# One set of strip buffers for a whole three-stage kernel, and conversions and products bound to new places

## The chip, the cores and the metric

The kernel runs on one core of one Trainium2 chip. The metric is device time in microseconds for one execution; the time before is the median of three runs.

## What is computed

Banded attention with four sink columns, then a layer that mixes over tokens and over channels, then the real part of a 2-D Fourier transform, a layer norm and a two-layer MLP. The weights come to the chip as pairs of 32-bit words.

```python
def _attn_ref(q, k, v, n_sink, window):
    scores = scale * np.matmul(q, k.transpose(0, 1, 3, 2))
    keep = is_sink | in_window
    scores = np.where(keep, scores, -1000000000.0)
...
    return np.matmul(a, v).astype(np.float32)

def _moe_ref(x, w_theta, w_tok_r, w_tok_i, w_ch):
    theta = x @ w_theta
    cos_t, sin_t = (np.cos(theta), np.sin(theta))
    zr = x * cos_t
    zi = x * sin_t
    yr = np.einsum('ts,bsd->btd', w_tok_r, zr)
    yi = np.einsum('ts,bsd->btd', w_tok_i, zi)
    u = x + yr + yi
    return u + np.maximum(u @ w_ch, 0.0)

def _moe2_ref(x, w_ch1, w_ch2):
    u = x + np.real(np.fft.fft(np.fft.fft(x, axis=1), axis=2))
...
    ch = np.maximum(un @ w_ch1, 0.0) @ w_ch2
    return (u + ch).astype(np.float32)
```

Two batches, 8 heads of 64, 768 rows, a window of 128; the model width is 512 and the MLP's hidden width 2048.

## The kernel before, in words

**Attention** goes through 12 tiles of 128 rows (2 batches of 6), each in four steps of two heads. A step makes scores on PE, masks them and takes the maximum on DVE (L518), the exponential on ACT (L522), transposes the probabilities on PE into `tp` (L229), evicts them with `rnd` (DVE L210 or ACT L208) and multiplies with v into `oa`; L597 to L599 normalise. In between, `theta_gen` (L765 to L794) makes theta of a finished tile in `th`; its phase is reduced on ACT (L788), DVE (L789, L790) and POOL (L791).

**Sine and cosine** of a tile (b, i) are three ACT instructions in `trig_act` (L800 sine, L801 absolute value, L802 cosine) and two products with x in `trig_mul` (L809), on DVE or POOL.

**Token mixing** (`y_gen`, once for each batch) goes through six tiles j, with a half step for the cosine product and one for the sine product of each. A product is split into a high part (ACT L208) and a low part (L214; DVE for batch 0, POOL for batch 1), and a half step is 24 matmuls into `bank` and three `acc` (512 columns) and two `pc` (256 columns). The generator pauses twice in each half step, so `rest` counts four pauses n for each tile. After this, `chain` runs channel mixing and the Fourier transform (`dft_gen`) of batch 0 between the half steps of batch 1; then comes the MLP.

**Weights** arrive in strips: one DMA, or two, on SP's queue fill a raw buffer of 128x1024 words. `conv` (L270) turns one strip into 128x512 float32: ACT rescales the high words in place (L282), DVE puts the bits together in three steps (L290, L291, L294). Where `self.room` is set, the scratch of the middle steps is a PSUM tile `s`; otherwise it is the target itself, `t`, in SBUF. `split` and `weight_split` make a high and a low part (ACT L208, POOL L214). Token weights have three strips for each tile j, issued in the order 0, 2, 1.

**What sets the order.** Tile's scheduler lays the instructions out on each engine by a model of times and by dependences that only set order. `paced(lag, ref)` gives what is issued inside it such a dependence on a given instruction, or on the matmul `lag` back; `issue_after` does the same for the trigonometry. `pump` (L324) converts the next strip that has been fetched, and then `ahead` (L319) issues further ones as raw buffers are free.

**Raw buffers before.** Attention has three (`raw0` to `raw2`, in its own pool, L397), and stage two opens three others (`rawb0` to `rawb2`, L1176). By 113.11 us the DMAs of all strips of token weights 0 to 3 have been issued, and the strips of weights 0 to 2 are converted within attention. The three strips of weight 3 lie in `raw` until stage two opens; it converts them at once, with PSUM scratch (the loop at L1178), and only then fetches weights 4 and 5 and the channel strips through `rawb`. In `rest`, the pauses n below 2, and those with n mod 4 in `P3S = (1, 3)`, convert one strip each, paced 24 matmuls back.

Of the kernel before, what the change touches and what calls it, by code (L numbers as in the profile page):

```python
# [11 lines left out]
F32 = mybir.dt.float32  # L12
# [23 lines left out]
NRAW1 = 3  # L36
# [13 lines left out]
P3S = (1, 3)  # L50
# [142 lines left out]
class _Body:  # L193
# [11 lines left out]
    def rnd(self, eng, o, i):  # L205
        nc = self.nc
        if eng == "a":
            nc.scalar.activation(o, i, AF.Copy)  # L208
        else:
            nc.vector.tensor_copy(o, i)  # L210
# [137 lines left out]
    def start(self):  # L348
# [17 lines left out]
        self.q, self.v, self.vs, self.ks, self.raw = {}, {}, {}, {}, deque()  # L366
# [28 lines left out]
    def open_attention(self, e, banded):  # L395
        nc = self.nc
        self.raw = deque(e.tile([128, 1024], F32, name=f"raw{k}") for k in range(NRAW1))  # L397
# [136 lines left out]
    def turn(self, n, hp):  # L534
# [20 lines left out]
        self.rnd("v" if tail else EPT[hp], pt[:, 0:k], tp[:, 0:k])  # L555
        self.pt[n, hp] = pt, [(u, m) for u, _, m in parts]
        if hp == 3 and i >= 2:
            tp = self.ps_tp.next()
            self.tr(tp[:, 0:128], self.pt.pop((n, 5)).rearrange("p h c -> p (h c)"), self.ident)
            pst = self.pst.next()  # L560
            self.rnd("v" if tail else "a", pst, tp[:, 0:128])
            self.pt[n, 4] = pst
# [44 lines left out]
    def attn_banded(self):  # L607
        last = len(self.seq) - 1
        nc = self.nc
        self.tn, self.pt, self.scs = {}, {}, {}  # L610
# [4 lines left out]
        for s in range(nstep + T0 + AL + 4):  # L615
# [33 lines left out]
            if s in (nstep + 1, nstep + 3):  # L649
                u = (s - nstep) // 2  # L650
                with self.tc.issue_after(self.last_exp):
                    self.trig_act(0, u)
                self.trig_mul(0, u, "v")
# [27 lines left out]
            elif P0B <= s < P0E and s % P0N == 0:  # L681
                self.pump(12, lag=0, ref=self.last_exp)
            if LA:
                self.mark(LA)
# [120 lines left out]
    def trig_mul(self, b, i, eng="p"):  # L805
        x = self.x.pop((b, i))
        e = self.nc.vector if eng == "v" else self.nc.gpsimd
        for t in self.z[b, i]:
            e.tensor_tensor(t, x, t, op=ALU.mult)  # L809
# [338 lines left out]
    def all(self, banded):  # L1148
# [17 lines left out]
        with ExitStack() as ctx:  # L1166
# [9 lines left out]
            self.raw = deque(e.tile([128, 1024], F32, name=f"rawb{k}") for k in range(NRAW))  # L1176
            self.room = self.ps_s
            for _ in range(len(self.fetched)):  # L1178
                key, raw = self.fetched.popleft()
                self.w[key] = self.conv(raw)  # L1180
            self.raw = deque(list(self.raw)[0:NRAW])
            self.ahead(DEPTH)
            self.room = None
# [7 lines left out]
    def rest(self):  # L1191
        self.sz = self.s.carve(6)
        yg = self.y_gen(0)
        for n, _ in enumerate(yg):
# [8 lines left out]
            if u == 0 and j + 2 < NS:  # L1203
                self.trig_tile(0, j + 2, "v")
            if u == 2 and j < 2:
# [3 lines left out]
            if n < 2 or u in P3S and n < 22:  # L1209
                self.pump(14, lag=24)  # L1210
# [151 lines left out]
```

## Time and profile before

| what | value |
|---|---|
| median of three runs | 619.36 us (617.69 to 619.75) |
| the profiled execution | 619.76 us |
| its span | 617.6 us |
| PE, PE's weight loads | 96%, 84% of the span |
| DVE, ACT, POOL | 57%, 56%, 48% |
| DMA moved | 46.61 MB, mean 75 GB/s |

The profiled execution's own time is 2.2 us above its span and 0.4 us above the median. Busy shares are averages over three stages with different limits. A row of a timeline gives start, busy time, engine, line of the kernel, operation and tile, and in brackets how long the engine was idle before and what released it. The granted clock is a share of PE's full speed. A wait counts where PE, the busiest engine, is the one that waits.

### The profile page before, as it was taken

How to read it: one execution, taken by the hardware profiler on the slowest of the kernel's cores; microseconds unless marked ns; L12 is line 12 of the kernel's file. 1: busy time of each engine (PE TensorE's matmuls, PEld its weight loads, DVE VectorE, ACT ScalarE, POOL GpSimd, SP SyncE). 2: the span in 40 equal slices, each digit the busy share in tenths (PEclk: the TensorE clock that was granted, in tenths of full speed). 3: DMA queues.
4: the chain of work that ended last, by engine and by line, in shares of the span. 5: the costliest groups of instructions: out<-in, count | busy, mean ns of one | idle time of the engine just before them, and what ended most of it. 6: DMA issues, size and time to landing. Idle time of an engine off the chain costs nothing.

```text
span 617.6 us, 9541 instructions
## 1 busy us (share of the span) xinstructions
PE 594.4 (96%) x3490; PEld 521.8 (84%) x3490; DVE 351.4 (57%) x734; ACT 343.2 (56%) x790; POOL 296.4 (48%) x252
## 2 busy tenths in 40 slices
PE   8989999989959999998999999999999999999996
PEld 6868878778848899987899999898899889989985
DVE  5777777754999786585886646746334211121112
ACT  4576766792856443556788854337457433343340
POOL 1122231232845443514565666548758456556551
PEclk9999999999969999998999999999999999999999
DMA  7843351200235612412256710100000000010001
GB/s 245 310 137 120 91 167 54 85 2 1 102 103 162 188 35 70 136 34 70 69 175 195 206 38 2 53 0 1 1 0 27 28 1 1 1 51 1 1 1 57
DMA packets 23337, 46.61 MB, mean 75 GB/s; under 512 B 2512, under 2 KB 9552, under 8 KB 23280
## 3 DMA queue, kind: packets, MB, share of 16 engines
q1 hardware_dynamic: 22032, 43.74, 22.3%
q0 software_dynamic: 1248, 2.17, 1.3%
q8 instruction: 29, 0.48, 0.3%
q14 instruction: 28, 0.23, 0.1%
HBM read 42.75 MB, written 3.15 MB: 74 GB/s over the span
## 4 chain that ended last, share of the span: by engine, by line
PE 81%; DVE 8%; ACT 5%; DMA 2%; issue 1%; SPq 0%; ACTq 0%; DVEq 0%
PE pc L224 26%; PE acc L224 23%; PE s L224 9%; PE bank L224 8%; PE th L224 4%; PE oa L224 4%; PE tp L229 3%; ACT p L522 2%; PE s L229 2%; PE sc L224 2%; DMA raw<-in_w_theta_dram 1%; DVE t L809 1%; ACT t L208 1%; DVE t L290 1%; DVE sc L518 1%
## 5 line engine op out<-in xcount | busy, mean ns | idle before, releaser
L214 POOL TENSOR_TENSOR t<-t 128x512 fp32r<-128x512 f32 x151 | 200.6, 1345 | 185.3 <-ACT t L208 164.3
L224 PE MATMUL pc<-t 128*128 128x384 f32 (+1 forms) x1056 | 199.6, 324 | 0.4 <-ACT t L208 0.4
L224 PEld LDWEIGHTS pc<-t 128*128 128x128 f32 x1056 | 181.6, 189 | 12.1 <-ACT t L208 0.6
L224 PE MATMUL acc<-t 128*128 128x512 f32 x648 | 181.4, 399 | 0.5 <-ACT t L1119 0.5
L208 ACT ACTIVATE t<-t 128x512 fp32r<-128x512 f32 x172 | 102.5, 626 | 98.2 <-PE acc L224 30.2
L224 PEld LDWEIGHTS acc<-t 128*128 128x128 f32 x648 | 117.5, 190 | 19.3 <-ACT t L1119 0.9
L1120 DVE SCALAR_TENSOR_TENSOR t<-pc,t 128x384 fp32r<-128x384 f32 x64 | 35.5, 555 | 130.3 <-ACT t L1119 130.2
L214 POOL TENSOR_TENSOR t<-xT,t 128x512 fp32r<-128x512 f32 x39 | 50.9, 1313 | 53.2 <-ACT xT L775 29.4
L224 PE MATMUL bank<-t 128*128 128x512 f32 x216 | 67.6, 409 | 7.9 <-ACT t L208 6.9
L224 PE MATMUL s<-t 128*128 128x256 f32 (+3 forms) x492 | 69.2, 285 | 0.9 <-DVE st L1040 0.9
L224 PEld LDWEIGHTS s<-t 128*128 128x128 f32 x492 | 65.2, 190 | 3.5 <-DVE st L1040 1.1
L1119 ACT ACTIVATE t<-pc 128x384 fp32r<-128x384 f32 x64 | 31.1, 488 | 57.7 <-PE pc L224 53.3
L224 PEld LDWEIGHTS bank<-t 128*128 128x128 f32 x216 | 39.8, 193 | 16.5 <-ACT t L208 7.9
L224 PEld LDWEIGHTS oa<-t 128*128 128x128 f32 x352 | 45.7, 193 | 2.1 <-ACT p L522 0.8
L224 PE MATMUL oa<-t 128*128 128x64 f32 x352 | 46.8, 264 | 0.4 <-DMA t<-in_v_dram 0.4
L522 ACT ACTIVATE p<-sc,nb 128x272 f32<-128x272 f32 (+1 forms) x72 | 33.1, 468 | 12.8 <-DVE nb L518 12.5
L791 POOL TENSOR_TENSOR t<-t 128x512 f32<-128x512 f32 x12 | 15.6, 1302 | 48.9 <-DVE t L790 41.6
L224 PE MATMUL th<-t 128*128 128x512 f32 x132 | 37.2, 414 | 0.0
L282 ACT ACTIVATE rawb<-rawb 128x512 f32<-128x512 f32 x42 | 28.3, 674 | 12.4 <-DMA rawb<-in_w_ch_dram 7.8
L229 PE MATMUL tp<-ident,p 128*128 128x128 f32 x176 | 33.6, 280 | 0.4 <-DVE t L210 0.4
L518 DVE CUSTOM_DVE_ANT_0 sc<-sc,m 128x272 f32<-128x272 f32 (+1 forms) x72 | 28.6, 443 | 2.7 <-PE sc L224 2.7
L224 PEld LDWEIGHTS th<-t 128*128 128x128 f32 x132 | 23.5, 188 | 7.8 <-issue 2.6
(144 smaller groups left out, 728.2 us busy)
## 6 DMA issues: line engine op xcount, KB each, us to landing
rawb<-in_w_ch_dram SPq DMA_DIRECT2D x36, 512.0 KB, 4.0
kst<-in_k_dram SPq DMA_DIRECT2D x12, 256.0 KB, 3.5
t<-in_v_dram SPq DMA_DIRECT2D x12, 256.0 KB, 4.6
out_dram<-t SPq DMA_DIRECT2D x12, 256.0 KB, 2.5
t<-in_q_dram SPq DMA_DIRECT2D x11, 256.0 KB, 4.7
raw<-in_w_theta_dram SPq DMA_DIRECT2D x4, 512.0 KB, 6.8
raw<-in_w_tok_rT_dram SPq DMA_DIRECT2D x4, 512.0 KB, 3.6
raw<-in_w_tok_iT_dram SPq DMA_DIRECT2D x4, 512.0 KB, 3.9
```

The source lines that it names most:

```text
L208: nc.scalar.activation(o, i, AF.Copy)
L214: e.tensor_tensor(o, x, hi.bitcast(F32), op=ALU.subtract)
L224: i = self.nc.tensor.matmul(o, lhsT=lhsT, rhs=rhs, start=start, stop=stop, skip_group_check=True).ins
L229: self.chained(self.nc.tensor.transpose(o, x, ident).ins)
L282: nc.scalar.activation(hf, hf, AF.Copy, scale=2.0 ** -112)
L290: nc.vector.tensor_scalar(t, hi, 3, None, op0=ALU.logical_shift_left)
L518: nc.vector.tensor_tensor_reduce(out=sc[:, 0:wd], in0=sc[:, 0:wd], in1=mask, op0=ALU.add, op1=ALU.min, scale=-0.125, scalar=3.0e38, accum_ ...
L522: self.last_exp = nc.scalar.activation(p[:, h, 0:wd], sc[:, 0:wd], AF.Exp, bias=nb[:, h:h + 1], scale=-1.0, accum_out=sm[:, h:h + 1]).ins
L791: nc.gpsimd.tensor_tensor(ph, km, ph, op=ALU.subtract)
L809: e.tensor_tensor(t, x, t, op=ALU.mult)
L1119: nc.scalar.activation(hh, hp, AF.Relu)
L1120: self.hl = nc.vector.scalar_tensor_tensor(hl, in0=hp, scalar=0.0, in1=hh.bitcast(F32), op0=ALU.max, op1=ALU.subtract).ins
```

## The change

There is one set of raw buffers for the whole program; `rawb` and the loop that converted the lying strips at stage two's opening are gone. `rnd` returns its instruction, and attention records its evictions in `ev`. In attention's last steps (`TAIL`, counted from the end of the scores) one strip is converted behind each of three evictions, and a split of token weight 1 is issued one step later. The products of tiles (0,0) and (0,1) are bound behind evictions of the last tile. In `rest`, nine pauses (`YC`) convert one strip each, bound behind the last product issued (`tm`), and the splits of the next tile's token weight are issued there too. Lines of the changed kernel are 1 lower up to about L360 and about 5 higher from `theta_gen` on.

```diff
     def rnd(self, eng, o, i):
         nc = self.nc
         if eng == "a":
-            nc.scalar.activation(o, i, AF.Copy)
-        else:
-            nc.vector.tensor_copy(o, i)
+            return nc.scalar.activation(o, i, AF.Copy).ins
+        return nc.vector.tensor_copy(o, i).ins
...
-NRAW1 = 3
-P3S = (1, 3)
+TAIL = (2, 4, 6)
+YC = (1, 3, 5, 9, 11, 13, 17, 19, 21)
...
+        self.raw = deque(cst.tile([128, 1024], F32, name=f"raw{k}") for k in range(NRAW))
...
-        self.raw = deque(e.tile([128, 1024], F32, name=f"raw{k}") for k in range(NRAW1))
...
-        self.rnd("v" if tail else EPT[hp], pt[:, 0:k], tp[:, 0:k])
+        self.ev[n, hp] = self.rnd("v" if tail else EPT[hp], pt[:, 0:k], tp[:, 0:k])
...
                 with self.tc.issue_after(self.last_exp):
                     self.trig_act(0, u)
-                self.trig_mul(0, u, "v")
+                with self.paced(ref=self.ev[last, 1 + u]):
+                    self.trig_mul(0, u, "v")
...
+            if s - nstep in TAIL:
+                self.pump(12, ref=self.ev[last, 1 + (s - nstep) // 2])
+            elif s - nstep - 1 in TAIL:
+                with self.paced():
+                    self.weight_split("tok", 1, TAIL.index(s - nstep - 1))
...
         for t in self.z[b, i]:
-            e.tensor_tensor(t, x, t, op=ALU.mult)
+            self.tm = e.tensor_tensor(t, x, t, op=ALU.mult).ins
...
-            self.raw = deque(e.tile([128, 1024], F32, name=f"rawb{k}") for k in range(NRAW))
-            self.room = self.ps_s
-            for _ in range(len(self.fetched)):
-                key, raw = self.fetched.popleft()
-                self.w[key] = self.conv(raw)
-            self.raw = deque(list(self.raw)[0:NRAW])
             self.ahead(DEPTH)
-            self.room = None
...
             if u == 0 and j + 2 < NS:
                 self.trig_tile(0, j + 2, "v")
+                tm = self.tm
...
-            if n < 2 or u in P3S and n < 22:
-                self.pump(14, lag=24)
+            if n in YC:
+                self.pump(14, ref=tm)
+            if u < 3 and j + 1 < NS:
+                with self.paced(lag=24):
+                    self.weight_split("tok", j + 1, (0, 2, 1)[u])
```

**First place: DVE at the end of attention.** `tp` holds transposed probabilities; t_1499 and t_563 are the two products of tile (0,0), t_1520 and t_665 those of tile (0,1). Before:

```order
L598 RECIPROCAL rs1_180<-rs1_180 128x8
L809 TENSOR_TENSOR t_1499<-t_322,t_1499 128x512
L809 TENSOR_TENSOR t_1520<-t_426,t_1520 128x512
L809 TENSOR_TENSOR t_563<-t_322,t_563 128x512
L210 COPY t_1358<-tp0_206 128x512
L210 COPY pst0_171<-tp1_207 128x128
L789 TENSOR_SCALAR t_1382<-t_1381 128x512
L809 TENSOR_TENSOR t_665<-t_426,t_665 128x512
```

With the change:

```order
L597 RECIPROCAL rs1_180<-rs1_180 128x8
L209 COPY t_1358<-tp0_206 128x512
L209 COPY pst0_171<-tp1_207 128x128
L794 TENSOR_SCALAR t_1382<-t_1381 128x512
L795 TENSOR_SCALAR t_1382<-t_1382 128x512
L209 COPY t_1400<-tp1_207 128x512
L213 TENSOR_TENSOR t_1392<-xT1_71,t_1391 128x512
L598 TENSOR_TENSOR t_1432<-oa0_208,rs0_179 128x512
L209 COPY t_1421<-tp0_206 128x512
L814 TENSOR_TENSOR t_563<-t_322,t_563 128x512
L814 TENSOR_TENSOR t_1499<-t_322,t_1499 128x512
```

The two copies stand directly behind the reciprocal, and the products of tile (0,0) come behind two further copies and a normalisation.

**Second place: DVE in the first token mixing.** t_748 is the cosine product of tile (0,2), t_848 that of (0,3) and t_1282 that of tile (1,1); t_1624, in the changed kernel t_1633, is the sine product of (0,2). Before:

```order
L809 TENSOR_TENSOR t_848<-t_646,t_848 128x512
L291 SCALAR_TENSOR_TENSOR t_1630<-rawb0_1559,t_1630 128x512
L290 TENSOR_SCALAR t_1648<-rawb1_1560 128x512
L294 SCALAR_TENSOR_TENSOR t_1630<-rawb0_1559,t_1630 128x512
L290 TENSOR_SCALAR s1_1552<-rawb2_1561 128x512
L291 SCALAR_TENSOR_TENSOR t_1648<-rawb1_1560,t_1648 128x512
L809 TENSOR_TENSOR t_1624<-t_531,t_1624 128x512
L809 TENSOR_TENSOR t_1282<-t_1104,t_1282 128x512
L291 SCALAR_TENSOR_TENSOR s1_1552<-rawb2_1561,s1_1552 128x512
L214 TENSOR_TENSOR t_1886<-t_848,t_1885 128x512
L294 SCALAR_TENSOR_TENSOR t_1648<-rawb1_1560,t_1648 128x512
L809 TENSOR_TENSOR t_748<-t_531,t_748 128x512
```

With the change:

```order
L814 TENSOR_TENSOR t_1633<-t_531,t_1633 128x512
L289 TENSOR_SCALAR t_1651<-raw1_109 128x512
L290 SCALAR_TENSOR_TENSOR t_1651<-raw1_109,t_1651 128x512
L289 TENSOR_SCALAR s0_1582<-raw2_110 128x512
L814 TENSOR_TENSOR t_748<-t_531,t_748 128x512
L293 SCALAR_TENSOR_TENSOR t_1651<-raw1_109,t_1651 128x512
L814 TENSOR_TENSOR t_1714<-t_646,t_1714 128x512
L290 SCALAR_TENSOR_TENSOR s0_1582<-raw2_110,s0_1582 128x512
L794 TENSOR_SCALAR t_1628<-t_1627 128x512
L289 TENSOR_SCALAR s1_1583<-raw0_108 128x512
L213 TENSOR_TENSOR t_1785<-t_748,t_1784 128x512
```

The products of tiles (0,3) and (1,1) now follow those of (0,2), and three conversion steps stand between the two products of (0,2); before, seven conversion steps and two products of other tiles stand ahead of its cosine product in this piece. The steps that write to t have their scratch in SBUF, those that write to s in PSUM.

**Third place: ACT in the same stretch.** t_1282, t_848 and t_748 are first the phases and then the cosines of the same three tiles. Before:

```order
L800 ACTIVATE t_1763<-t_1282 128x512
L282 ACTIVATE rawb0_1559<-rawb0_1559 128x512
L802 ACTIVATE t_848<-t_848,hpi_68 128x512
L282 ACTIVATE rawb1_1560<-rawb1_1560 128x512
L801 ACTIVATE t_1282<-t_1282 128x512
L282 ACTIVATE rawb2_1561<-rawb2_1561 128x512
L800 ACTIVATE t_1624<-t_748 128x512
L802 ACTIVATE t_1282<-t_1282,hpi_68 128x512
L208 ACTIVATE t_1885<-t_848 128x512
L801 ACTIVATE t_748<-t_748 128x512
L208 ACTIVATE t_1959<-t_1630 128x512
L802 ACTIVATE t_748<-t_748,hpi_68 128x512
```

With the change:

```order
L805 ACTIVATE t_1633<-t_748 128x512
L208 ACTIVATE t_1742<-t_1180 128x512
L806 ACTIVATE t_748<-t_748 128x512
L281 ACTIVATE raw1_109<-raw1_109 128x512
L281 ACTIVATE raw2_110<-raw2_110 128x512
L807 ACTIVATE t_748<-t_748,hpi_68 128x512
L805 ACTIVATE t_1714<-t_848 128x512
L208 ACTIVATE t_1768<-t_1244 128x512
L793 ACTIVATE t_1627<-s1_1583 128x512
L806 ACTIVATE t_848<-t_848 128x512
L281 ACTIVATE raw0_108<-raw0_108 128x512
L208 ACTIVATE t_1784<-t_748 128x512
```

The sine, absolute value and cosine of tile (0,2) have moved ahead of those of (0,3).

## Rows read from the trace of the kernel before

**Rows 1.** The page: busy shares; PE and its clock in 40 slices
```profile
PE 594.4 (96%) x3490; PEld 521.8 (84%) x3490; DVE 351.4 (57%) x734; ACT 343.2 (56%) x790; POOL 296.4 (48%) x252
...
PE   8989999989959999998999999999999999999996
...
PEclk9999999999969999998999999999999999999999
```

**Rows 2.** Timeline of PE, 130 to 146 us; start, us, what
```profile
136.73 0.66 PE L229 MATMUL tp<-ident,t 128*128 128x128 f32 x4 [1.97 <-DVE t L210]
```

**Rows 3.** Timeline of PE, 169.6 to 188 us
```profile
179.67 1.22 PE L224 MATMUL bank<-t 128*128 128x512 f32 x2 [6.92 <-ACT t L208]
```

**Rows 4.** Busy by stretch: PE, PEld, DVE, ACT, POOL; clock, DMA
```profile
137.00:141.00 4.00, 4.00 (x19) 2.97 (x18) 3.04 (x6) 2.64 (x5) 1.59 (x1) 0.61 0.00 0
141.00:145.00 4.00, 4.00 (x21) 3.21 (x20) 2.49 (x4) 0.00 (x0) 0.00 (x0) 0.97 0.00 0
...
180.00:186.00 6.00, 6.00 (x20) 4.99 (x20) 6.00 (x9) 3.09 (x7) 3.06 (x3) 0.53 0.51 162
...
281.00:285.00 4.00, 4.00 (x16) 3.44 (x16) 1.48 (x3) 3.55 (x8) 1.66 (x3) 0.57 0.47 133
```

**Rows 5.** Timeline of DVE, 130 to 146 us
```profile
135.38 0.69 DVE L809 TENSOR_TENSOR t<-t 128x512 f32<-128x512 f32 x1 [0.96 <-ACT t L802]
135.99 0.68 DVE L210 COPY t<-tp 128x512 f32<-128x512 f32 x1
```

**Rows 6.** Busy time by stretch, DVE alone
```profile
155.00:172.00 17.00, 16.78 (x21) 1.00 0.26 93
172.00:202.00 30.00, 29.26 (x39) 0.83 0.49 142
```

**Rows 7.** Timeline of DVE, 161 to 180 us
```profile
170.38 0.68 DVE L291 SCALAR_TENSOR_TENSOR t<-rawb,t 128x512 int32<-128x512 int32 x1
...
173.12 3.43 DVE L809 TENSOR_TENSOR t<-t 128x512 f32<-128x512 f32 x2
...
178.27 0.68 DVE L809 TENSOR_TENSOR t<-t 128x512 f32<-128x512 f32 x1
```

**Rows 8.** Timeline of ACT, 167 to 180 us
```profile
172.64 0.70 ACT L802 ACTIVATE t<-t,hpi 128x512 f32<-128x512 f32 x1
```

**Rows 9.** Timeline of POOL, 135 to 202 us
```profile
172.81 3.18 POOL L214 TENSOR_TENSOR t<-t 128x512 fp32r<-128x512 f32 x2 [2.91 <-PE s L224]
```

**Rows 10.** Busy time by stretch, POOL alone
```profile
135.00:157.00 22.00, 5.44 (x4) 0.92 0.00 1
```

**Rows 11.** Timeline of SP's queue, 100 to 215 us
```profile
159.80 0.80 SPq L258 DMA_DIRECT2D rawb<-in_w_tok_rT_dram  x2
...
186.44 2.73 SPq L258 DMA_DIRECT2D rawb<-in_w_ch_dram  x2
```

**Rows 12.** Instructions of one tile, rawb: its DMAs
```profile
DMA to landing us min/median/max: 2.7/3.9/6.0
```

**Rows 13.** Groups by line, 140 to 216 us; busy, mean ns, idle
```profile
L294 DVE SCALAR_TENSOR_TENSOR t<-rawb,s 128x512 int32<-128x512 int32 x10 | 6.8, 678 | 0.2
```

**Rows 14.** Timeline of PE, 199 to 213 us
```profile
199.31 0.86 PE L224 MATMUL bank<-t 128*128 128x512 f32 x3
...
203.51 0.86 PE L224 MATMUL bank<-t 128*128 128x512 f32 x3
```

**Rows 15.** Timeline of DVE, 196.5 to 209 us
```profile
197.91 0.68 DVE L214 TENSOR_TENSOR t<-t 128x512 fp32r<-128x512 f32 x1
```

**Rows 16.** Timeline of PE, 270 to 292 us
```profile
279.09 0.81 PE L229 MATMUL s<-ident,xT 128*128 128x128 f32 x4 [0.86 <-ACT Y L1025]
280.80 1.34 PE L224 MATMUL s<-t 128*128 128x256 f32 x6 [0.90 <-DVE st L1040]
```

**Rows 17.** Timeline of ACT, 196.5 to 209 us
```profile
201.10 0.68 ACT L282 ACTIVATE rawb<-rawb 128x512 f32<-128x512 f32 x1 [0.66 <-DMA rawb<-in_w_ch_dram]
...
204.39 0.68 ACT L282 ACTIVATE rawb<-rawb 128x512 f32<-128x512 f32 x1 [1.58 <-DMA rawb<-in_w_ch_dram]
```

More of the change, by code (lines that the diff above doesn't have):

```diff
@@ L365, in start @@
         self.s.grow(ctx.enter_context(tc.tile_pool(name="g", bufs=1)), NSLOT)
-        self.q, self.v, self.vs, self.ks, self.raw = {}, {}, {}, {}, deque()
+        self.q, self.v, self.vs, self.ks = {}, {}, {}, {}
+        self.raw = deque(cst.tile([128, 1024], F32, name=f"raw{k}") for k in range(NRAW))
         early = [self.xT[b].rearrange("p a s -> p (a s)") for b in range(B)]
@@ L560, in turn @@
             pst = self.pst.next()
-            self.rnd("v" if tail else "a", pst, tp[:, 0:128])
+            self.ev[n, 4] = self.rnd("v" if tail else "a", pst, tp[:, 0:128])
             self.pt[n, 4] = pst
@@ L609, in attn_banded @@
         nc = self.nc
-        self.tn, self.pt, self.scs = {}, {}, {}
+        self.tn, self.pt, self.scs, self.ev = {}, {}, {}, {}
         th = {}
```

## The prediction

> **What bounds the kernel now.** First the page's busy shares and its 40 slices: PE is busy 594.4 us, 96% of the span, so nothing shorter than PE's own work is to be had and a change of order can win only the waits of PE and the stretches in which its clock is at half [rows 1]. The reader should see the one slice (the twelfth, near 170 to 185 us) in which the PE digit is 5 and the clock digit 6 [rows 1]. Second, the timeline of PE where this change works. It has two waits worth a name. Near 135 us, in attention's last steps, PE waits 1.97 us for a DVE copy (L210) [rows 2]. At 172.75 us, in the first token mixing, it waits 6.92 us for an ACT split (L208) before `bank` [rows 3]. Third, the windows: the granted clock is 0.61 in the 4 us behind the first wait and 0.53 in the 6 us behind the second [rows 4], which is the lower of the levels 1.2 and 2.4 GHz for most of them. So each wait costs twice. The ceiling is 1.97 + (1-0.61)x4 = 3.53 us and 6.92 + (1-0.53)x6 = 9.74 us, 13.3 us in all.
>
> Fourth, the engine behind each. Near 135 us DVE runs a product (L809, 135.38) before the copy at 135.99 that PE wants; that product itself waited 0.96 us for ACT's cosine, and the copy stood behind it in the queue, while PE had nothing to do but wait for it [rows 5]. Near 172 us DVE is busy without a break: 16.78 of 17 us, then 29.26 of 30 [rows 6]. There conversions of the strips (L290, L291, L294) and products (L809) stand in one queue, and the cosine product that PE needs next, that of tile (0,2), is the last of them at 178.27 [rows 7]. Its cosine left ACT at 172.64 + 0.70 = 173.3 us [rows 8], so 5 us of the wait are pure queue on DVE. One more thing shows: a product takes about 1.7 us (two at 173.12 take 3.43) while POOL runs its L214 (3.18 us from 172.81 on), and 0.68 (178.27) when POOL rests [rows 7, 9].
>
> **The change part by part.**
>
> *Products of tiles (0,0) and (0,1) bound behind the last copies.* Two COPYs now come ahead of L809, and the sine and cosine products stand behind them (first place in the order). PE's transposes are fed by the copy as soon as ACT and PE have done their part. Removed: 1.97 us of wait and its clock, 3.53 us. The products are wanted only by the first token mixing, which stands behind attention and theta in the new order of PE, so a later start of four times 0.69 costs nothing there; if that cover were gone, the price would be 4 x 0.69 = 2.8 us.
>
> *Three strips converted in attention's last steps.* Before, the strips of token weight 3 are fetched early and then lie until stage two opens, where nine DVE instructions convert them. Now each is converted behind an eviction in attention's tail. Nine instructions of about 0.68 us are 6.1 us of DVE and three prescalings of ACT some 0.67 each; DVE does 3.04 us of 4 behind the first wait, ACT 2.64 and nothing in the 4 us after [rows 4], so there is room, and PE waits for none of it. The splits of weight 1 come with them on ACT (0.6 us each) and POOL, which works 5.44 of 22 us there [rows 10]. A raw buffer is free as soon as it is converted, so SP issues the strips of weights 4 and 5 from attention's tail on, eight issues, and then the channel strips, which SP sent off from 186.44 on [rows 11]. Behind them in SP's queue stands one load of a DFT table, which nobody needs before the DFT; the q, k and v loads are all ahead. I cost the moved DMAs at nothing: the cover is the time from landing to use (the four issues at 159.80 and behind belong to strips that PE uses from 199.31 on), and without it each would cost a landing of 3.9 us [rows 12].
>
> *The conversions of stage two, one at a time behind a product.* In the second place of the order the cosine product of tile (0,2) (t_748) has two products and four conversion steps fewer ahead of it, and its ACT steps (third place) come before those of tile (0,3). With nine conversion steps less in this queue (9 x 0.6 = 5.4 us by start-to-start times) the product starts more than the 5 us earlier that were queue, and the rest of the wait, ACT's late cosine, is shortened by its own move forward. Removed: 9.74 us, and at least 5 + 0.47x6 = 7.8 if ACT's 1.9 stays.
>
> *One price the trace does not show.* These four conversions (three in the tail, one behind the first product) write to SBUF scratch and not to PSUM scratch (before, two did). The two steps of each with two SBUF inputs were seen only with POOL at rest, 0.68 us (170.38), against 1.7 for a product of two SBUF inputs beside POOL [rows 7]; the form with PSUM scratch keeps to 678 ns in the mean of ten, POOL working beside some [rows 13]. So eight steps cost between 0 and 8 x (1.7 - 0.68) = 8.2 us more of DVE. I take 8.2 x 5.44/22 = 2 us, by POOL's share there [rows 10], none of it on PE's path, and keep both ends. The Trainium skill (SBUF — State Buffer, section "SBUF: two separate sides") says that such a step and a GpSimd step lock each other out whole, one after the other; by that rule the eight would come to the upper end if POOL worked all along, and the removed 9.74 would shrink by as much. The trace agrees in that products are slow only beside POOL [rows 7, 9].
>
> *What then is late.* PE that gains 13.3 us arrives earlier at everything that follows, and DVE's solid list [rows 6] moves up only by what left it. A half step of 24 matmuls takes 203.51 - 199.31 = 4.20 us [rows 14]. The low part of the sine of tile (0,4) ended at 197.91 + 0.68 = 198.59 [rows 15], PE used it at 203.51: slack 4.9 us. The feeding chain moves up by D, at least 0 and at most 3.53 + 5.4 = 8.9 us. I choose D = 3.6: the clock and wait of the tail reach DVE's start, the nine steps are largely filled by products that now wait for their ACT steps. Then 4.9 + 3.6 = 8.5 of the 13.3 us come through to the end of token mixing; the rest returns as smaller waits near 195 to 205 us. One of them will again drop the clock, as at 281, where 0.57 was granted for 4 us and (1-0.57)x4 = 1.7 us went [rows 4]. 8.5 - 1.7 = 6.8 us.
>
> *Behind it.* In the DFT groups PE waits 0.86 and 0.90 us before 279.09 and 280.80 for a chain of ACT and DVE [rows 16]. There the new order of DVE puts one conversion step more between two steps of this chain, 0.6 us, and the channel strips fall at other places; one more drop of the clock is 1.7. I set 2.3 us of loss; the ends are -1.8 (both waits gone) and +4.6 (two such steps, each with a drop). Sum: 6.8 - 2.3 = 4.5 us. The profiled execution took 619.76 us, of which the span is 617.6; the forecast is 615.2 against it, and against the median of 619.36, 0.4 lower, **614.8 us**.
>
> **The rivals.**
>
> *Nearly all of it stays.* The list of DVE moves up by the whole 8.9 us, and the slack of 4.9 covers the rest: 13.3 less some dips, 9 to 13 us, 606.4 to 610.4. For it: PE's waits behind 215 us are small. Against it: DVE without a break to 202 us [rows 6].
>
> *All is given back.* DVE's work for tiles (0,3) to (0,5) is the same, with eight steps dearer (8.2 us at most), and the time saved at 172 us is waited for at 190 to 205. Then D is 0, 4.9 us come through, two drops and the DFT groups take 1.7 + 1.7 + 0.9 or more: within 1.9 us of the median. That is also how it ends if the change doesn't do what it says, the products being held by ACT's order all the same.
>
> *Slower: ACT's one queue behind a strip's DMA.* With one set of three buffers a channel strip can be issued only when the buffer's last reader is done. At the end of token mixing the prescale (L282) of a channel strip stands in ACT's order right ahead of the splits of the sine of tile (0,4) and the cosine of tile (0,5). Before, ACT waits 0.66 and 1.58 us at such prescales for the DMA [rows 17], and PE doesn't feel it. A strip takes 3.9 us from issue to landing [rows 12]. If PE comes 13.3 us earlier to the sine of tile (0,4), at 203.5 - 13.3 = 190.2, and the strip before it lands later, PE waits up to 3.9 us at each of two places, with 1.7 to 2 us of clock each, 11 to 12 us; with 4.5 us of gain set against it and the DFT's 2.3 staying away or not, the kernel ends 3 to 7 us slower, 622 to 626. It decides when the landing is later than 190 us less the prescale, split and low part, some 2 us. For it: before, such strips were issued from 186.44 on [rows 11] and land 3.9 us later, at 190.3. Against it: the buffers are free earlier, so all strips are issued earlier.
>
> **How the numbers follow.** Forecast 0.50 (its own range, D between 2 and 6 and the DFT term between 0 and 4.5, is 612.3 to 617.4); nearly all stays 0.10; given back 0.24; slower 0.16. The range reaches 610.0, which takes in the edge of the second case, and 621.5, which takes in the third and leaves most of the slower one out. A measurement of this kernel can tell about 0.3% (1.9 us) from no change: faster by more 0.60, within it 0.24, slower 0.16.
>
> **What would show it.** Right: no wait over 0.5 us of PE near 135; the wait near 172 under 2 us; the slices' clock digit 6 gone there; new waits of 1 to 3 us between 190 and 206, released by ACT L208 or POOL; the token mixing's end some 7 us earlier; one or two us lost again between 260 and 295. Wrong: the wait before `bank` of tile (0,2) still over 5 us (then ACT's order was the cause, not DVE's queue); products or conversions of 1.7 us in attention's tail; ACT idle over 2 us on a strip's DMA directly before a wait of PE (the slower rival); or the whole 13 us still there at 215 us.

## The result and the profile after

The changed kernel takes 612.38 us (median of six runs, 611.54 to 612.94); the kernel before took 619.07 in the same comparison. The ratio is 0.9895, with a 95% interval of 0.9877 to 0.9913: faster by 1.05%, more than the 0.3% that can be told from no change. The forecast was 614.8 us, in a range of 610.0 to 621.5. The profiled execution took 612.40 us, its span is 610.6.

The page of the changed kernel, the lines of [rows 1]:

```profile
PE 592.3 (97%) x3490; PEld 518.4 (85%) x3490; DVE 349.9 (57%) x731; ACT 343.8 (56%) x793; POOL 301.1 (49%) x252
...
PE   8989999998899999989999999999999999999996
...
PEclk9999999999899999999999999999999999999999
```

The slice with PE at 5 and the clock at 6 is gone; in its place the tenth and eleventh slices (137 to 168 us) show 8, and the clock 8 in the eleventh. The spans by stretch show where the time went. The cuts are the same events in both kernels: the first and the last masked score in `sc`, the first row of token mixing's sum (`xT<-bank`), the first row `Y` of the Fourier transform, the first step of the MLP. First the kernel before (columns: stretch; its length; busy time of PE, PEld, DVE, ACT, POOL; granted clock; DMA):

```profile
7.00:128.30 121.30, 118.54 (x816) 94.21 (x817) 89.73 (x304) 83.73 (x272) 28.08 (x22) 1.00 0.45 146
128.30:212.80 84.50, 75.62 (x427) 64.89 (x426) 67.49 (x100) 49.73 (x91) 40.87 (x34) 0.92 0.33 98
212.80:274.00 61.20, 60.78 (x422) 56.12 (x420) 45.91 (x65) 29.17 (x50) 24.12 (x21) 1.00 0.25 74
274.00:311.00 37.00, 34.44 (x200) 30.24 (x200) 26.05 (x50) 26.86 (x69) 17.22 (x20) 0.95 0.21 63
311.00:617.60 306.60, 299.31 (x1609) 271.85 (x1608) 119.33 (x202) 152.20 (x311) 184.14 (x152) 1.00 0.13 42
```

The changed kernel:

```profile
7.50:129.70 122.20, 119.85 (x828) 95.59 (x827) 90.37 (x305) 82.30 (x270) 28.31 (x23) 1.00 0.45 144
129.70:205.40 75.70, 72.01 (x416) 61.55 (x415) 58.90 (x91) 47.13 (x89) 43.41 (x33) 0.98 0.30 93
205.40:266.60 61.20, 61.11 (x422) 56.33 (x420) 50.34 (x69) 32.21 (x54) 25.82 (x22) 1.00 0.26 87
266.60:304.10 37.50, 34.06 (x201) 28.60 (x200) 28.06 (x54) 28.28 (x69) 16.98 (x20) 1.00 0.24 76
304.10:610.60 306.50, 299.00 (x1609) 271.53 (x1609) 119.29 (x202) 152.42 (x311) 184.55 (x152) 1.00 0.13 42
```

The end of attention with the first token mixing is 8.8 us shorter (84.5 to 75.7), and everything behind it keeps its length within 0.5 us; 11 or 12 matmuls have moved into the first stretch, which is 0.9 longer and begins 0.5 later. At the end of the first token mixing the changed kernel is 212.8 - 205.4 = 7.4 us ahead, and 7.0 at the end of the span.

Between 130 and 270 us PE now has four waits of over 0.25 us:

```profile
138.21 0.73 PE L223 MATMUL th<-t 128*128 128x512 f32 x2 [0.76 <-ACT t L208]
...
146.10 0.66 PE L228 MATMUL tp<-ident,t 128*128 128x128 f32 x4 [0.52 <-DVE t L209]
...
153.24 0.49 PE L223 MATMUL bank<-t 128*128 128x512 f32 x1 [0.97 <-ACT t L208]
155.17 0.72 PE L223 MATMUL bank<-t 128*128 128x512 f32 x2 [1.44 <-POOL t L213]
```

Neither the 1.97 us of [rows 2] nor the 6.92 us of [rows 3] is left. The place near 135 has a wait of 0.76 at 138.21, and there is no wait over 0.25 us from 156 to 270 us. New is the entry into token mixing: 0.97 us for ACT and 1.44 us for POOL, and behind them a stretch at a lower clock:

```profile
155.00:160.00 5.00, 4.83 (x20) 4.32 (x21) 1.79 (x2) 0.75 (x2) 4.25 (x6) 0.66 0.36 105
```

(1-0.66)x5 = 1.7 us of clock, 4.1 us with the two waits. That entry is where most of the missing gain went: of the 13.3 us that the two old waits cost, 4.1 are lost here, 0.76 + 0.52 = 1.3 in the new waits before it, and 0.5 by the later start of the first stretch, which leaves 7.4. At the Fourier transform PE still has three waits (0.88 before 271.78, 0.90 before 273.49, 1.07 before 281.04). The first two are those of [rows 16], the third was 0.79 before 289.33; the clock behind them is now 1.00 in the traced execution.

**Behind the entry wait.** PE waits for the split of weight 1 on ACT, and ACT for POOL:

```profile
152.04 2.19 ACT L208 ACTIVATE t<-t 128x512 fp32r<-128x512 f32 x4 [4.16 <-POOL t L796]
```

```profile
137.46 1.27 POOL L796 TENSOR_TENSOR t<-t 128x512 f32<-128x512 f32 x1 [4.14 <-DVE t L795]
147.66 4.35 POOL L796 TENSOR_TENSOR t<-t 128x512 f32<-128x512 f32 x1 [8.93 <-DVE t L795]
153.32 4.64 POOL L213 TENSOR_TENSOR t<-t 128x512 fp32r<-128x512 f32 x3 [1.31 <-issue]
```

The subtraction L796 at 147.66 takes 4.35 us, the one ten microseconds earlier 1.27. What DVE does in that time:

```profile
147.76 0.68 DVE L293 SCALAR_TENSOR_TENSOR t<-raw,t 128x512 int32<-128x512 int32 x1
148.37 0.68 DVE L290 SCALAR_TENSOR_TENSOR t<-raw,t 128x512 int32<-128x512 int32 x1
148.97 0.68 DVE L213 TENSOR_TENSOR t<-xT,t 128x512 fp32r<-128x512 f32 x1
149.57 0.68 DVE L290 SCALAR_TENSOR_TENSOR t<-raw,t 128x512 int32<-128x512 int32 x1
150.17 0.68 DVE L293 SCALAR_TENSOR_TENSOR t<-raw,t 128x512 int32<-128x512 int32 x1
150.78 0.68 DVE L598 TENSOR_TENSOR t<-oa,rs 128x512 f32<-128x512 f32 x1
```

Five instructions in a row with both inputs in SBUF: conversion steps of the tail (L293, L290) and one low part (L213). The last of them ends near 150.8, where L598 begins, which reads its first input from PSUM; POOL's instruction ends 1.2 us after that, at 152.0, about as long as it took at 137.46. Each DVE step keeps its 0.68 us. So it was POOL that stood still, for some 3.1 us. ACT's split then starts at 152.04; the scheduler had it wait for POOL alone, with the three splits of weight 1 queued behind it. The trace leaves three links to be shown: that the slow subtraction is the cause, that ACT waits for a place and not for data, and that each part of the change is worth what the prediction said. The runs below show the first two; the third they show in part.

### The profile page after: what moved, and what is told of

It is laid out like the page before. It is cut to its first block, busy times and chain, and to the rows that moved or that the text cites. A ratio compares the mean times of both kernels' runs of the same rounds, so it can differ in the third digit from the quotient of the medians.

```text
span 610.6 us, 9548 instructions
## 1 busy us (share of the span) xinstructions
PE 592.3 (97%) x3490; PEld 518.4 (85%) x3490; DVE 349.9 (57%) x731; ACT 343.8 (56%) x793; POOL 301.1 (49%) x252
## 4 chain that ended last, share of the span: by engine, by line
PE 61%; DVE 8%; ACT 4%; issue 1%; POOL 1%; ACTq 0%; DVEq 0%; POOLq 0%
PE pc L223 23%; PE acc L223 21%; PE s L223 8%; PE bank L223 7%; PE s L228 2%; ACT t L208 1%; DVE t L213 1%; DVE t L293 1%; ACT raw L284 1%; ACT raw L281 1%; ACT t L1060 1%; DVE t L931 1%; DVE t L285 1%; POOL t L213 1%; DVE t L1045 0%
## 5 line engine op out<-in xcount | busy, mean ns | idle before, releaser
L213 POOL TENSOR_TENSOR t<-t 128x512 fp32r<-128x512 f32 x151 | 201.8, 1353 | 172.8 <-ACT t L208 154.9
L213 POOL TENSOR_TENSOR t<-xT,t 128x512 fp32r<-128x512 f32 x39 | 51.5, 1328 | 54.8 <-ACT xT L780 30.3
L223 PE MATMUL bank<-t 128*128 128x512 f32 x216 | 65.2, 399 | 3.4 <-POOL t L213 1.4
L281 ACT ACTIVATE raw<-raw 128x512 f32<-128x512 f32 x58 | 39.3, 680 | 13.7 <-DMA raw<-in_w_ch_dram 9.3
L796 POOL TENSOR_TENSOR t<-t 128x512 f32<-128x512 f32 x12 | 18.8, 1565 | 48.2 <-DVE t L795 41.3
```

Source lines behind the costliest of these rows:

```text
L213: e.tensor_tensor(o, x, hi.bitcast(F32), op=ALU.subtract)
L223: i = self.nc.tensor.matmul(o, lhsT=lhsT, rhs=rhs, start=start, stop=stop, skip_group_check=True).ins
L281: nc.scalar.activation(hf, hf, AF.Copy, scale=2.0 ** -112)
L796: nc.gpsimd.tensor_tensor(ph, km, ph, op=ALU.subtract)
```

## The experiments

Each ratio is to the kernel before in runs of the same round, whose medians are 618.92 to 619.46 us. The last column is read from one traced execution of each.

| run | us, median | to before, 95% interval | end of the first token mixing |
|---|---|---|---|
| before | 619.07 | 1 | 212.8 |
| changed kernel | 612.38 | 0.9895 [0.9877, 0.9913] | 205.4 |
| products bound, alone | 615.91 | 0.9947 [0.9930, 0.9963] | 209.4 |
| change without the binding of products | 615.67 | 0.9949 [0.9931, 0.9967] | 207.5 |
| change without conversions in the tail | 613.24 | 0.9895 [0.9874, 0.9915] | 205.9 |
| change with unbound conversions | 615.76 | 0.9939 [0.9921, 0.9957] | 208.9 |
| change without early splits | 614.08 | 0.9925 [0.9907, 0.9943] | 206.9 |
| change, one subtraction on DVE | 609.60 | 0.9853 [0.9831, 0.9874] | 202.1 |
| change, a place kept | 611.73 | 0.9878 [0.9858, 0.9899] | 204.0 |
| change, four subtractions on DVE | 609.91 | 0.9856 [0.9838, 0.9875] | 202.0 |
| change, two steps joined, one tile | 610.66 | 0.9867 [0.9842, 0.9892] | 202.0 |
| change, two steps joined, four tiles | 609.55 | 0.9843 [0.9821, 0.9865] | 201.5 |

**One part alone: the products bound behind the last copies.** On the kernel before:

```diff
...
-                self.trig_mul(0, u, "v")
+                with self.paced(ref=self.ev[last, 1 + u]):
+                    self.trig_mul(0, u, "v")
```

> The kernel before with one part of the change alone: the products of tiles (0,0) and (0,1) are bound behind the last tile's copies. Theory: the wait of 1.97 us near 135 goes, with its half clock, 3.5 us; DVE's list of stage two begins when attention ends, moves up with it, and the wait of 6.9 us before bank stays as long as it is: 615.8 us (615 to 617). Rival: the list does not move up, the wait before bank grows from 6.9 to about 10 us, and the time is 619 (618 to 620).

Measured 615.91, 3.55 us below the median of 619.46 in its round (by the interval 2.3 to 4.3). The wait near 135 is gone, and the one in token mixing is as long as in [rows 3], 3.2 us earlier:

```profile
176.49 1.22 PE L223 MATMUL bank<-t 128*128 128x512 f32 x2 [6.96 <-ACT t L208]
```

The theory holds. DVE's list moved up with attention's end, and the term of 3.53 us stands within the interval; the traces put the end of the first token mixing 212.8 - 209.4 = 3.4 us earlier.

**The same part undone in the changed kernel.**

```diff
-                with self.paced(ref=self.ev[last, 1 + u]):
-                    self.trig_mul(0, u, "v")
+                self.trig_mul(0, u, "v")
```

> The changed kernel without the binding of the products of tiles (0,0) and (0,1) behind the last copies; all else stays. On DVE one product comes ahead of the two copies, not three. Theory (the wait of 3.5 us at attention's end is a term of its own, as the run with the binding alone showed): PE waits 1 to 2 us near 135 again, with some half clock behind it, 614 to 616 us. Rival (the entry takes it): PE would only come earlier to the wait at 151 to 155, which shrinks by what it loses at 135, and the time stays within 1 us of 612.4.

The time is as the theory said, 615.67, by luck: its mechanism is wrong. At 134.77 PE waits only 0.45 us. It waits in another place, the matmuls of a theta tile:

```profile
154.26 4.64 PE L223 MATMUL th<-t 128*128 128x512 f32 x10 [4.42 <-DVE t L213]
```

Here the order on POOL and DVE came out another way. POOL does its subtraction at 145.28 in 1.28 us and then meets the conversions with its three low parts of weight 1; now DVE's steps are the slow ones, and one of them is the low part of theta's input:

```profile
145.28 1.28 POOL L795 TENSOR_TENSOR t<-t 128x512 f32<-128x512 f32 x1 [6.88 <-DVE t L794]
```

```profile
149.11 1.76 DVE L290 SCALAR_TENSOR_TENSOR t<-raw,t 128x512 int32<-128x512 int32 x1
150.80 1.75 DVE L293 SCALAR_TENSOR_TENSOR t<-raw,t 128x512 int32<-128x512 int32 x1
152.47 1.74 DVE L213 TENSOR_TENSOR t<-xT,t 128x512 fp32r<-128x512 f32 x1
```

Three steps of 1.75 us where the changed kernel has 0.68. POOL's three low parts, at 148.86 to 153.7, take 1.47 to 1.68 us, so here the two engines took turns. It is the same clash, lost mostly by the other side: of PE's 4.4 us it makes up some 3 x 1.07 = 3.2.

**The conversions of the tail taken out.** The strips of weight 3 are converted when stage two opens, with PSUM scratch, and weight 1 is split in token mixing:

```diff
-TAIL = (2, 4, 6)
+TAIL = ()
...
+            self.room = self.ps_s
+            for _ in range(len(self.fetched)):
+                key, raw = self.fetched.popleft()
+                self.w[key] = self.conv(raw)
             self.ahead(DEPTH)
+            self.room = None
```

> The changed kernel without its conversions in attention's tail: the three strips of weight 3 are converted when stage two opens, with PSUM scratch, as before, and weight 1 is split in token mixing; the one raw set, the bound products and the bound conversions stay. Theory of the sum (DVE's list bounds the first token mixing, and the nine steps that left it, 5.4 us, are what carries the gain): waits of PE between 165 and 200 us come back, 4 to 6 us with the half clock that follows, 616 to 619 us. Rival (the order of the products is enough): the cosine product of tile (0,2) comes in time all the same, waits under 1.5 us, and since no two-SBUF steps lock POOL out at the tail's end the time is 608.5 to 612.5.

Measured 613.24, between the two and not to be told from the changed kernel by time alone. The wait comes back, at 2.86 us in place of 6.92, and with it the clock (0.50 and 0.65 in the eight microseconds from 172 on):

```profile
172.81 1.22 PE L223 MATMUL bank<-t 128*128 128x512 f32 x2 [2.86 <-ACT t L208]
```

That is 2.9 us of wait and 3.0 of clock (counted from 172.81 on), nearly 6. The entry wait of 4.1 us is gone in exchange. No conversion stands beside POOL's subtraction now, and the one that took 4.35 us takes 1.27:

```profile
146.56 1.27 POOL L796 TENSOR_TENSOR t<-t 128x512 f32<-128x512 f32 x1 [8.83 <-DVE t L795]
```

Both theories were half right; the conversions in the tail are worth some 6 us and cost 4. The difference of 2 us is that of the two traced executions, 614.32 and 612.40.

**The conversions of token mixing not bound behind a product.**

```diff
-                self.pump(14, ref=tm)
+                self.pump(14, lag=24)
```

> The changed kernel, but the nine conversions in the first token mixing are paced 24 matmuls back, as before, and not bound behind a product. On DVE six conversion steps and a product of another tile now stand ahead of the cosine product of tile (0,2), where the changed kernel has four. Theory (the binding carries part of the gain): PE waits 1 to 4 us before bank of tile (0,2), 613.5 to 617 us. Rival (nine steps less in the list are enough, the product has slack): no wait over 0.5 us there and 612.4, within 1 us.

Measured 615.76: without the binding 3.4 us are lost. But PE waits at another tile than expected. The cosine product of (0,2) comes in time; the wait is at the cosine of tile (0,4), for its low part, with a clock of 0.61 in the four microseconds behind:

```profile
194.25 0.50 PE L223 MATMUL bank<-t 128*128 128x512 f32 x1 [1.91 <-DVE t L213]
```

The low part begins at 193.52, directly behind a product that took 6.20 us on DVE, where the slowest product of the changed kernel near there took 2.22 (187.02). POOL ran its low parts, each at its usual 1.3 us, until 193.0:

```profile
187.39 6.20 DVE L814 TENSOR_TENSOR t<-t 128x512 f32<-128x512 f32 x1
```

```profile
186.16 2.57 POOL L213 TENSOR_TENSOR t<-t 128x512 fp32r<-128x512 f32 x2
...
189.25 3.79 POOL L213 TENSOR_TENSOR t<-t 128x512 fp32r<-128x512 f32 x3
```

So the clash shows once more, and this time DVE got no turn. The loss comes from what stood beside the product in the new order, not from conversion steps ahead of it.

**The splits of the next weight not issued in token mixing.**

```diff
-            if u < 3 and j + 1 < NS:
-                with self.paced(lag=24):
-                    self.weight_split("tok", j + 1, (0, 2, 1)[u])
```

> The changed kernel without the splits of the next token weight that are issued in token mixing 24 matmuls back; they are issued at the start of each tile, and the scheduler then puts those of weights 2 and 3 earlier on ACT, five of them ahead of the phase of the last theta but one. Theory (ACT's queue matters here too): the sine and cosine of tile (0,2) come some 3 us later, PE waits 1 to 4 us before bank of tile (0,2), 613.5 to 617 us. Rival (ACT has that much slack): 612.4 within 1 us.

Measured 614.08, in the theory's range without its wait: nothing over 0.25 us at tile (0,2), so ACT has that slack, as the rival said, and the time is in the range by luck. The waits at the entry are those of the changed kernel (0.98 and 1.44), but the clock around them is lower: 0.80, 0.50 and 0.85 in the twelve microseconds from 152 on, where the changed kernel has 0.99, 0.59 and 1.00. That is 1.7 us, the whole difference. Why the clock fell further is not settled.

**The cause of the entry wait: the subtraction moved to DVE.**

```diff
-        nc.gpsimd.tensor_tensor(ph, km, ph, op=ALU.subtract)
+        (nc.vector if 6 * b + i == 9 else nc.gpsimd).tensor_tensor(ph, km, ph, op=ALU.subtract)
```

> The changed kernel, but one instruction is moved from POOL to DVE: the subtraction of the phase (L796) of tile (1,3), which in the trace of the changed kernel took 4.35 us on POOL at 147.66 where the one at 137.46 took 1.27. Theory (lock): DVE ran conversion steps with two SBUF inputs in that time and POOL could not get at SBUF; the ACT split behind it in its queue waited 4.16 us for POOL, and PE 0.97 and 1.44 us, with a granted clock of 0.66 over 5 us (1.7 us). Then with the subtraction as one DVE step of about 0.7 us, ACT's wait there falls under 1.5 us, the two waits of PE to under 1 us together, and the time to 608.5 us (607.0 to 610.5). Rival (entry): PE comes early to the first token mixing and what it waits for is the three low parts of weight 1 on POOL, 1.5 us each in a row; then the wait of PE before bank stays at 2 us or more and the time within 1 us of 612.4. Second rival: the added DVE step holds up a copy in attention's tail, and PE waits over 1 us there, 613 to 615.

Measured 609.60, 2.8 us below the changed kernel, and the two intervals against before do not overlap. Four of the five runs took 609.16 to 609.71 us, the fifth 612.12. ACT's split waits 1.86 us and not 4.16, and begins 2.1 us earlier:

```profile
149.94 2.19 ACT L208 ACTIVATE t<-t 128x512 fp32r<-128x512 f32 x4 [1.86 <-DVE t L796]
```

```profile
150.50 2.60 PE L223 MATMUL th<-t 128*128 128x512 f32 x10 [0.41 <-DVE t L213]
152.94 0.97 PE L223 MATMUL bank<-t 128*128 128x512 f32 x3
```

Both waits before `bank` are gone; one of 0.41 us has come, at a theta matmul behind DVE's added step. No lower clock follows. The theory holds; its 1.5 us for ACT's wait was too small, with no effect.

**A place, not data.** The subtraction stays on POOL, and the place of its scratch is not handed on:

```diff
-        self.give(km)
         self.ph[b, i] = ph
+        if 6 * b + i != 9:
+            self.give(km)
+        else:
+            self.km = km
...
+        if not hasattr(self, 'km_done'):
+            self.km_done = self.give(self.km)
         fill = self.chain(0, self.ps_s)
```

> The changed kernel, but the scratch place that the slow POOL subtraction (L796 of tile (1,3)) reads is not given back before channel mixing. The subtraction stays on POOL. Theory (a place, not data): the ACT split that waited 4.16 us at 152.04, the high part of the cosine product of tile (0,1), needs nothing that this subtraction makes; it waited because its target lies in the place that the subtraction still read. Then POOL's subtraction is still over 3 us long, ACT's split does not wait for it, and PE's waits of 0.97 and 1.44 us before bank shrink to under 1 us together, 608.5 to 610.5 us. Rival: ACT or POOL is held by the subtraction all the same, since POOL's low parts of weight 1 stand behind it in POOL's own queue; then 1.4 us or more of PE's wait for POOL stays, 611 to 613.

POOL is as slow as before, and the split does not care:

```profile
148.17 4.35 POOL L796 TENSOR_TENSOR t<-t 128x512 f32<-128x512 f32 x1 [8.92 <-DVE t L795]
```

```profile
145.62 0.63 ACT L208 ACTIVATE t<-t 128x512 fp32r<-128x512 f32 x1 [0.32 <-PE oa L223]
```

It runs at 145.62, before the subtraction begins, and that one ends at 152.5; ACT needed only the place. PE's 2.4 us have become 0.41 at a theta matmul, as in the run before, and 0.63 for POOL, whose low parts stand behind the slow subtraction (the releaser L1182 is a small fill that follows the first of them):

```profile
152.49 1.72 POOL L213 TENSOR_TENSOR t<-t 128x512 fp32r<-128x512 f32 x1
```

```profile
154.26 0.73 PE L223 MATMUL bank<-t 128*128 128x512 f32 x2 [0.63 <-POOL bs L1182]
...
195.04 0.50 PE L223 MATMUL bank<-t 128*128 128x512 f32 x1 [0.68 <-DVE t L213]
```

So both were right in part: a place for ACT, its own queue for POOL. The time, 611.73, lies in the rival's range and 1.2 us above the theory's. The traced execution, with 612.51 the slowest of the four (610.57 to 612.51), shows two things that came back later: 0.68 us at 195.04 (above) and a clock of 0.58 from 272 to 276, 1.7 us, behind waits that are no longer than the changed kernel's. The wait at 195.04 is at the sine of tile (0,4), and behind it stands the chain of the slower rival. ACT stood 3.11 us for the DMA of a channel strip, and the splits came after it:

```profile
191.88 0.66 ACT L281 ACTIVATE raw<-raw 128x512 f32<-128x512 f32 x1 [3.11 <-DMA raw<-in_w_ch_dram]
```

```profile
193.61 1.38 DVE L213 TENSOR_TENSOR t<-t 128x512 fp32r<-128x512 f32 x1 [1.91 <-ACT t L208]
```

**Versions that go further.** Four subtractions on DVE in place of one (`6 * b + i >= 8`):

> The changed kernel with the phase subtraction of the last four tiles, (1,2) to (1,5), on DVE and not on POOL. Theory: only that of tile (1,3) met the row of two-SBUF conversion steps; the other three were 1.27 to 1.68 us on POOL off PE's path, so this is as fast as the kernel with one of them moved, 609.6 (608.5 to 610.5). Rival: three steps more in DVE's list of the first token mixing, 2 us, make PE wait at the sine of tile (0,2) or later, 611 to 613.

609.91: no more and no less than one. Then the second rounding step and the subtraction in one DVE instruction, for one tile and for four (`== 9`, `>= 8`):

```diff
-        nc.vector.tensor_scalar(km, km, MAGIC, None, op0=ALU.subtract)
-        nc.gpsimd.tensor_tensor(ph, km, ph, op=ALU.subtract)
+        if 6 * b + i >= 8:
+            nc.vector.scalar_tensor_tensor(ph, in0=km, scalar=MAGIC, in1=ph, op0=ALU.subtract, op1=ALU.subtract)
+        else:
...
```

> The changed kernel with two steps of the phase of tile (1,3) made one on DVE: the second rounding step (L795) and the subtraction (L796, POOL) become one DVE instruction with two inputs, 0.69 us in place of 0.42 on DVE and 4.35 on POOL. Theory (lock, then place, then ACT's queue): as with the subtraction moved to DVE, no wait before bank over 0.5 us and no half clock near 156, and the instruction comes one step earlier, so PE's 0.41 us at the theta matmul of that run goes too: 609.2 us (608.3 to 610.0). Rival: it was worth less than a measurement tells, 609.6 to 610.4; the theory falls if a wait over 1 us is left between 145 and 160.

> The same joining of two steps for the tiles (1,2) to (1,5). Compared with the joining for one tile, DVE has 0.27 us more in each of three places and POOL three instructions less of 1.3 to 1.7 us. Theory: none of the three is on PE's path and the time is that of the single joining, 609.2 us within 0.8. Rival: POOL set free lets low parts of weights 1 and 2 come earlier and DVE meets less of POOL, so products shrink from 1.7 towards 0.7 us; since PE has no wait left between 155 and 200 this gives nothing in time either, but the products' mean there falls.

For one tile 610.66: no wait over 0.25 us is left between 147 and 260 in the traced execution, which is the fastest of the four (609.51; the others 610.36 to 611.15). Yet the median lies above the expected range; the interval takes in the 609.60 and overlaps with the changed kernel's. For four 609.55. The four versions can't be told from one another; all lie 1.3 to 1.6% below the kernel before. The mean of the ten products from 155 to 205 us did not fall with fewer POOL instructions (1134 ns against 1095 in the joining for one tile), so that rival falls.

## Why the prediction was right, and where it was not

*The wait at attention's end, 3.53 us:* right. Alone, the binding gives 3.55 us (2.3 to 4.3 by the interval), and the list of DVE moves up with it. In the whole change two smaller waits came in its place, 0.76 and 0.52 us, which the sum did not have.

*The wait before the third tile, 9.74 us:* right in size, and in cause as far as the runs go. It is gone from the changed kernel. With the nine steps back in DVE's queue 5.9 us of it return, 2.9 of wait and 3.0 of clock. The rest stays away in every run on the changed kernel; how much the order of the products and how much ACT's order carries is argued, not shown. The run with unbound conversions lost its time at the cosine of tile (0,4), one half step ahead of the place where the sum had set the next wait, through a product held up by POOL.

*D = 3.6 and the slack of 4.9:* near the measured value, for a wait that then didn't come. The low part of the sine of tile (0,4), from 197.91 on in [rows 15], now starts at 194.56; PE uses it at 196.08, not 203.51:

```profile
194.56 0.69 DVE L213 TENSOR_TENSOR t<-t 128x512 fp32r<-128x512 f32 x1 [0.56 <-ACT t L208]
```

```profile
196.08 0.86 PE L223 MATMUL bank<-t 128*128 128x512 f32 x3
```

D is 198.59 - 195.25 = 3.34 us. Of the 8.2 us that could pass there, 7.4 were used. Slack: 0.8 us. The run with one subtraction on DVE used up what is left:

```profile
192.29 0.69 DVE L213 TENSOR_TENSOR t<-t 128x512 fp32r<-128x512 f32 x1 [0.82 <-ACT t L208]
```

It ends at 192.98, with PE at that half step from 192.76 on; D is 5.6 us there. What holds it is not DVE's list alone, as the prediction had it: DVE stood idle 0.82 us for ACT's split, and ACT for the DMAs of two channel strips, 5.33 us and then

```profile
191.06 0.68 ACT L281 ACTIVATE raw<-raw 128x512 f32<-128x512 f32 x1 [1.00 <-DMA raw<-in_w_ch_dram]
```

with the split directly behind it, at 191.64. In the changed kernel the chain is the same:

```profile
191.40 0.69 ACT L281 ACTIVATE raw<-raw 128x512 f32<-128x512 f32 x1 [5.36 <-DMA raw<-in_w_ch_dram]
...
193.34 0.69 ACT L281 ACTIVATE raw<-raw 128x512 f32<-128x512 f32 x1 [0.73 <-DMA raw<-in_w_ch_dram]
193.92 1.66 ACT L208 ACTIVATE t<-t 128x512 fp32r<-128x512 f32 x3
```

The strips' DMAs are issued late because the buffer is freed late, by the last conversion step on DVE; SP's own waits in the changed kernel from 180 to 200 us say so (us in total, count, longest):

```profile
SPq L257 <- DVE t L293: 17.5, 6, 6.0
```

In the changed kernel that step ends at 185.22 + 0.67 = 185.89 and the first strip is issued at 185.96. So the bound is a ring: DVE's conversion, the freed buffer, the DMA, ACT's prescale, the split behind it, DVE's low part. The next gain in this stage has to open this ring somewhere; no run tried it.

*"None of it on PE's path":* this is the step that failed. The price of two-SBUF conversion steps beside POOL was bounded on DVE's side alone, 2 us of 8.2, and the question who waits if POOL is the one held up was not asked. The trace shows all eight of DVE's steps at 0.68 or 0.69 us, so of the 2 us nothing came, and POOL's subtraction at 4.35; by the place it held and ACT's queue, PE lost 0.97 + 1.44 + 1.7 = 4.1 us. The run with that subtraction on DVE gave 2.8 us back in the median. The rule that the prediction cited beside this step says it better than the step did: the Trainium skill (SBUF — State Buffer, section "SBUF: two separate sides") has whichever of the two starts first hold the shared ports and the other stand still. The traces agree that either side can stand still: in the changed kernel POOL did for 3.1 us, and in the run without bound products DVE took 1.75 us where it takes 0.68. Who gets the next turn they leave open. POOL's row begins at 147.66, ahead of the first of the five DVE steps at 147.76, and yet it got none between them; in the run with unbound conversions DVE's product got none between POOL's low parts; without the bound products the two took turns.

*The place of the smaller waits, 195 to 205 us, and one drop of the clock, 1.7 us:* wrong place, right amount, and the amount is luck. The drop came at 155 to 160 us and nothing was waited for later; 6.8 us were forecast for the end of the first token mixing, 7.4 came. The forecast took 8.5 us for what the slack lets through and 1.7 off; the slack was never used up, and what held the gain to 7.4 was above all the clash, which the sum had at nothing. Without the clash the lead there is 212.8 - 202.1 = 10.7 us.

*The Fourier transform, 2.3 us of loss:* mis-sized. The stretch is 0.5 us longer. Its clock rose from 0.95 to 1.00, which is some 1.8 us on 37, and PE's idle time there grew by 0.9 us (37.00 - 34.44 to 37.50 - 34.06), so half of what the better clock could give was waited for again; where the other half went the rows don't show. The 1.8 us between 2.3 and 0.5 are most of the difference between 614.8 and 612.4.

*The rivals:* "nearly all of it stays" named 606.4 to 610.4, and its range is reached once the clash with POOL is away (609.60), with D at 5.6 and not at its 8.9 us. "All is given back" fell. The slower rival's mechanism shows: ACT waits 2.31 us for a strip's DMA at 179.12 and 5.36 before 191.40. In the changed kernel it costs PE nothing, but it sets the 0.8 us of slack that are left, and in the run with a place kept it ends in PE's 0.68 us.

## What to carry to other kernels

When instructions of DVE with two SBUF inputs are packed into a stretch, look which POOL instruction lies in it and who waits for that, by data, by place in memory and by queue; price the clash on both engines, since either can lose. Undoing a part shows its net worth only: the conversions in the tail bring 6 us and cost 4 by the clash, and taking them out looked like 0.9, which is within the noise. And when a long wait is removed, the slack of each later use says how much can come through before the next chain bounds the stage; follow that chain back, which here runs through a DMA and a buffer and not only through the engine with the longest list.

## What was not expected

The granted clock in the Fourier transform doesn't follow from the waits that the trace names. The kernel before and the one with a place kept have 0.57 and 0.58 in four microseconds behind waits of about 0.9 us twice; the changed kernel has the same waits and 1.00. The same holds at the entry with 0.59 and 0.50 behind equal waits. One execution of each kernel was traced, and the clock is not the same in all executions of one kernel: its mean over the span is 0.994 to 0.999 in six of the changed kernel, and in the run with a place kept the execution at 0.999 took 610.57 us, those at 0.994 took 612.10 and 612.51. So the difference need not lie in the kernels at all. No run separates what decides it, and 1 to 2 us of any of these medians are open in that respect.
